# Six moves in a written-out order: an attention and expert-routing kernel on one core

## The chip, the cores and the metric

The kernel runs on 1 core of one Trainium2 chip. The metric is the device time of one execution in microseconds (us); less is better. The kernel before takes 195.74 us, the median of 3 runs (195.73 to 195.97).

## The reference

Two stages, one after the other. First an attention with pooled keys and values, for 8 batches of 8 heads, 576 queries and 64 columns a head; then a routed two-layer product of the 4608 rows that come out.

```python
k_p = k.reshape(B, H, 72, 8, D).mean(axis=3)          # 576 keys pooled to 72; v_p likewise
attn = softmax(q @ k_p.T / 8)
x = (attn @ v_p) as rows of 512                       # 576 rows for each batch
logits = normalized(x) @ normalized(expert_emb).T / tau
e = argmax(logits); gate = softmax(logits)[e]
out[row] = gate * (relu(x[row] @ w1[e]) @ w2[e])      # w1 512x1024, w2 1024x512, 8 experts
```

## The kernel before, in words

The kernel takes the 8 batches in turn and bets that all rows of a batch want one expert, which it guesses from the mean of the pooled values. It loads that expert's two weight arrays while the attention runs. A check at the end (`PR`, `PP`, `PX`) repeats a batch for which the guess was wrong.

Each batch is cut into steps, which are functions with a name and a batch number. Five lists in `TABLES` (L41 on), one for each of PE (TensorE), DVE (VectorE), ACT (ScalarE), POOL (GpSimd) and SP (SyncE), hold their names in the order in which that engine gets them. An engine runs its list strictly in order, so a step that waits holds up all that is behind it. `Plan.order` goes through the lists with an estimated time for each step; from that it takes two things only: which buffer a step gets (`Plan.free`: of the rings that the step allows, the slot that is reckoned free first), and how many dummy products (`keep_warm`, L959) are put ahead of a PE step in the first 62 us.

PSUM has two wide tiles (`pa`, 1024 columns, `psum`) and four narrow ones (`pb`, 512 columns, `bank`). Scores (`SC`) take both wide tiles at once; `PV` takes a wide one; all other PE steps take any of the six:

```python
tiles = [Buf(psum), Buf(psum)]          # SC
px = [Buf(psum)]                        # PV, from batch 1's on
p = Buf(bank, psum)                     # H, Y and the rest
```

The steps that the change and the prediction speak of, for batch b (`H3.4.0` is step H of batch 3, column block 4, row half 0):

- POOL: `V`, `K`, `Q`, `W1`, `W2` issue the loads of values, keys, queries and the two weight arrays; `PK` reads the guessed expert, which `GD` on DVE has found. `NA` takes the square root of the row norms (L446).
- DVE: `KA` and `KB` fold the 8 keys of a group into one (L506, L513), `VA` and `VB` the values. `QT` transposes queries (L605), four a batch. `KE` copies the transposed pooled keys (L632). `XM` divides the attention's output by its sums and gives x (L411, L412). `RE` finds the largest logit (L441 to L443), `NB` scales logits by the norms (L449 to L451), `ND` makes the gates.
- PE: `KT` transposes pooled keys (L616). `SC` makes scores from `KE` and `QT` (L646, L658). `PV` multiplies by the values (L725). `XT` transposes x (L420, L426). `RT` makes the logits (L435). `H` is a first-layer product of 4 matmuls (L822), `Y` a second-layer product for 128 rows (L834), `YL` that of the last 64 rows (L841).
- ACT and DVE share: `HE` takes the relu of an `H` out of PSUM (L828 on ACT, L830 on DVE), `XE` copies an `XT` (L743), `YE`, `YF` and `YG` scale a `Y` by its gate (L847, L849). A PSUM tile is free again only when this has been done.
- ACT alone: `EX` is the exponential of scores (L666, L674). `SQ` sums the squares of x (L754), one a chunk of rows; `NA` needs all five of a batch. `NC` is the exponential of logits (L813) and needs `NB`.

Batch 7, the last, has no work of a next batch beside it: its x is transposed by DMA (`XD`), and its 16 `H`, then `YL7` and the four `Y7`, end the kernel.

Of the kernel before, what the change touches and what calls it, by code (L numbers as in the profile page):

```python
# [44 lines left out]
H0.3.1 H0.4.1 GL1 H0.1.0 SC1.0.0 H0.0.1 H0.7.1 SC1.0.1 SC1.1.1 Y0.2 SC1.1.0 YL0 PV1.0 PV1.1 Y0.1  # L45
XT1.0 PV1.4 Y0.0 PV1.2 XT1.4 PV1.3 XT1.1 Y0.3 XT1.2 GM2 XT1.3 GL2 H1.5.0 H1.7.0 H1.4.0 H1.6.0
H1.5.1 H1.3.0 H1.1.0 H1.1.1 H1.2.0 KT2 RT1 H1.3.1 SC2.0 H1.4.1 H1.7.1 H1.2.1 H1.0.0 PV2.0 H1.0.1
H1.6.1 XT2.0 SC2.1 Y1.1 PV2.1 KT3 YL1 SC2.2 Y1.3 PV2.3 PV2.2 Y1.0 XT2.1 PV2.4 XT2.3 XT2.2 Y1.2
XT2.4 SC3.0 H2.2.0 RT2 H2.0.0 H2.1.0 H2.4.0 H2.0.1 H2.5.0 SC3.1 H2.5.1 H2.4.1 H2.2.1 H2.1.1
H2.6.0 GM4 GM3 H2.3.0 PV3.1 GL3 H2.7.0 H2.3.1 H2.6.1 H2.7.1 SC3.2 GL4 YL2 PV3.0 PV3.2 Y2.2 XT3.0  # L50
XT3.1 PV3.4 XT3.2 Y2.3 Y2.0 PV3.3 KT4 Y2.1 XT3.3 SC4.0 XT3.4 H3.3.0 H3.4.0 RT3 SC4.1 H3.2.0
H3.0.0 H3.3.1 H3.5.0 SC4.2 H3.1.0 H3.6.0 PV4.2 H3.7.0 H3.4.1 PV4.3 H3.1.1 PV4.0 H3.0.1 H3.6.1
H3.2.1 PV4.1 H3.7.1 XT4.0 H3.5.1 XT4.1 GM5 PV4.4 XT4.2 XT4.3 YL3 XT4.4 Y3.0 GL5 RT4 H4.7.0
H4.7.1 H4.5.0 H4.6.1 Y3.1 H4.5.1 Y3.2 Y3.3 H4.1.0 KT5 H4.6.0 H4.0.0 H4.3.0 SC5.0 H4.4.0 H4.0.1
# [8 lines left out]
""",  # L63
    "DVE": """
PRE GC0 GD0 VA0 QT0.0.0 QT0.0.1 KE0.0 KE0.1 QT0.1.0 QT0.1.1 VB0 XM0.0.0 XM0.1.0 XM0.0.1 XM0.1.1
XM0.3 XM0.2 XM0.4 VA1 VB1 RE0 GC1 KA1 KB1 HE0.5.1 KE1 QT1.0.0 QT1.0.1 GD1 QT1.1.0 QT1.1.1 GE0
HE0.0.1 HE0.1.1 NB0 ND0 YF0 XM1.0 XM1.1 VA2 XM1.4 VB2 KA2 XM1.2 XM1.3 GC2 KB2 HE1.5.0 XE1.3 GD2
HE1.4.0 QT2.0.0 QT2.0.1 QT2.1.1 QT2.1.0 KE2 RE1 HE1.3.1 NB1 HE1.1.1 XM2.0 GE1 KA3 KB3 XM2.1 ND1
QT3.0.0 QT3.0.1 QT3.1.1 KE3 XM2.3 YF1 XM2.2 XE2.1 XM2.4 QT3.1.0 XE2.2 VA4 VB4 RE2 HE2.0.0 GE2
HE2.4.0 HE2.1.0 HE2.5.0 VA3 VB3 NB2 GC4 GC3 GD3 XM3.1 HE2.3.1 HE2.6.1 ND2 GD4 YF2 XM3.0 QT4.0.0  # L70
XM3.2 QT4.0.1 KA4 XM3.4 KB4 QT4.1.0 XM3.3 QT4.1.1 KE4 YE2.1 XE3.3 XE3.4 RE3 HE3.4.0 VA5 VB5
XM4.2 HE3.0.0 XM4.3 XM4.0 XM4.1 XE4.0 HE3.5.1 NB3 XM4.4 QT5.0.0 GC5 GE3 QT5.1.0 ND3 RE4 GD5
QT5.1.1 QT5.0.1 YF3 KA5 VA6 HE4.5.0 VB6 KB5 HE4.6.1 GE5 KE5 VA7 HE4.3.0 NB4 YE3.3 HE4.4.0 KA6
GE4 HE4.1.1 ND4 QT6.0.0 KB6 YE4.3 GC6 QT6.1.1 YF4 XM5.2 XM5.0 GD6 XM5.4 XE5.0 XM5.1 KE6 XE5.2
XM5.3 QT6.1.0 VB7 QT6.0.1 HE5.5.0 HE5.2.0 RE5 QT7.0.0 HE5.1.0 GE6 QT7.1.1 GC7 GD7 HE5.4.0
# [19 lines left out]
XE5.3 YE4.1 EX6.0.0 EX6.0.1 HE5.5.1 SQ5.2 HE5.2.1 HE5.6.0 HE5.3.0 SQ5.0 EX6.1.0 HE5.4.1 EX6.1.1  # L95
HE5.3.1 HE5.7.0 HE5.0.0 HE5.1.1 HE5.0.1 SQ5.1 EX6.2.1 EX6.2.0 NC5 YE5.2 YG5 SQ6.2 XE6.2 SQ6.1
SQ6.3 YE5.0 XE6.4 SQ6.4 XE6.3 EX7.0.1 EX7.0.0 HE6.4.1 EX7.1.1 HE6.6.0 EX7.1.0 HE6.3.1 EX7.2.1
EX7.2.0 HE6.1.1 HE6.0.0 HE6.2.1 SQ6.0 NC6 SQ7.2 YE6.0 YE6.2 SQ7.1 HE7.3.0 HE7.6.0 YG6 SQ7.0
SQ7.3 SQ7.4 HE7.2.0 HE7.1.0 HE7.6.1 HE7.0.1 NC7 HE7.2.1 HE7.3.1 HE7.7.1 HE7.4.1 HE7.1.1 YG7
YE7.2 YE7.1.1  # L100
""",
    "POOL": """
V0.0 V0.1 K0.0 K0.1 Q0.0 Q0.1 V1.0 V1.1 PK0 W10 K1 Q1.0 W20 V2 K2 PK1 W11 Q2.0 NA0 K3 W21 Q3.0
# [1128 lines left out]
```

## Time and profile before

| what | value |
|---|---|
| median of 3 runs | 195.74 us |
| profiled execution | 196.42 us |
| its span | 194.6 us |
| PE busy | 186.9 us (96%), 2174 matmuls |
| DVE busy | 145.9 us (75%) |
| ACT busy | 126.6 us (65%) |
| POOL busy | 42.4 us (22%) |
| loads issued by POOL (q0) | 28.85 MB, 87.0% of 16 DMA engines' span |

The profile cuts the span into 40 equal slices; a digit is the busy share in tenths, and 9 is 90% or more:

```profile
PE   6999999999999999998999999999999999999991
DVE  1257888589978998879669999999798836863730
ACT  4017896776876998585987767727983787078410
PEclk9999999999999999999999999999999999999998
DMA  3999999999999999999999999999999991449843
```

PE counts as busy nearly throughout; matmuls overlap in the record, so what it loses shows only as short idle stretches ahead of single groups. PEclk is the granted clock of PE. The rest of the time between the span and the profiled execution's own time lies around the span.

### The profile page before, as it was taken

To read this page: it belongs to the slowest core of one execution; us is meant where nothing else is said; L and a number is where in the kernel's file an instruction comes from. 1 tells how busy PE (TensorE), PEld (TensorE's weight loads), DVE (VectorE), ACT (ScalarE), POOL (GpSimd) and SP (SyncE) were. 2 spreads that over 40 slices of the span, in tenths; PEclk is the share of its full clock that TensorE was granted. 3 is DMA by queue.
4 is the path that set the end of the run, shared out by engine and by line. 5 is a ranking of instruction groups with operands and counts; after the bars stand their busy time and mean duration, and the time that the engine had idled before them with its cause. 6 is when DMAs were issued, how large, how long until landed. Compare 5 with 4: busy or idle time off the path is not lost.

```text
span 194.6 us, 5502 instructions
## 1 busy us (share of the span) xinstructions
PE 186.9 (96%) x2174; PEld 127.2 (65%) x2175; DVE 145.9 (75%) x418; ACT 126.6 (65%) x288; POOL 42.4 (22%) x60
## 2 busy tenths in 40 slices
PE   6999999999999999998999999999999999999991
PEld 4775786556875677654786657667774778557651
DVE  1257888589978998879669999999798836863730
ACT  4017896776876998585987767727983787078410
POOL 7544000910371002350024332030140000202000
PEclk9999999999999999999999999999999999999998
DMA  3999999999999999999999999999999991449843
GB/s 38 179 207 202 206 212 206 179 207 208 209 208 210 207 211 203 141 191 206 214 196 218 261 212 226 249 192 203 251 262 231 214 317 63 97 148 344 298 138 115
DMA packets 30335, 39.30 MB, mean 202 GB/s; under 512 B 6616, under 2 KB 17112, under 8 KB 30304
## 3 DMA queue, kind: packets, MB, share of 16 engines
q0 software_dynamic: 21792, 28.85, 87.0%
q1 hardware_dynamic: 8288, 9.85, 15.5%
q8 instruction: 18, 0.29, 0.6%
q10 hardware_dynamic: 224, 0.20, 0.3%
q14 instruction: 13, 0.11, 0.2%
HBM read 61.88 MB, written 9.44 MB: 367 GB/s over the span
## 4 chain that ended last, share of the span: by engine, by line
PE 56%; DMA 19%; DVE 13%; issue 4%; POOL 3%; ACT 2%; POOLq 0%; DVEq 0%
PE pb L822 17%; DMA kr<-in_k_dram 15%; PE pb L834 13%; PE pa L834 4%; DMA qq<-in_q_dram 4%; PE pa L822 4%; DVE qT L605 3%; DVE x L412 3%; PE pa L658 3%; PE pa L725 3%; PE pb L841 2%; DVE kr L506 2%; PE pa L646 2%; PE pb L959 2%; POOL vr L362 1%
## 5 line engine op out<-in xcount | busy, mean ns | idle before, releaser
L822 PE MATMUL pb<-xt,w 128*128 128x288 f16 (+2 forms) x404 | 58.3, 286 | 0.2 <-ACT hT L828 0.2
L822 PEld LDWEIGHTS <-w 128*128 128x128 f16 x512 | 47.1, 98 | 13.6 <-issue 2.1
L834 PE MATMUL pb<-w,hT 128*128 128x512 f16 x208 | 48.7, 379 | 0.0
L834 PEld LDWEIGHTS <-hT 128*128 128x128 f16 x248 | 22.9, 98 | 24.8 <-issue 0.8
L666 ACT ACTIVATE at<-pa 72x792 f16<-72x792 f32 (+1 forms) x36 | 27.6, 803 | 9.4 <-PE pa L658 7.7
L828 ACT ACTIVATE hT<-pb 128x288 f16<-128x288 f32 (+2 forms) x66 | 24.9, 408 | 6.2 <-PE pb L822 5.4
L412 DVE TENSOR_TENSOR x<-pa,r_all 128x512 f16<-128x512 f32 x38 | 26.3, 691 | 1.4
L754 ACT ACTIVATE sq<-x 128x512 f16<-128x512 f16 x40 | 25.2, 629 | 1.5 <-DVE x L412 1.2
L605 DVE STREAM_TRANSPOSE qT<-qq 128x576 f16<-128x576 f16 x32 | 23.5, 758 | 2.0 <-DMA qq<-in_q_dram 2.0
L847 ACT ACTIVATE y<-pb,gm_all 128x512 f32<-128x512 f32 (+1 forms) x26 | 16.1, 627 | 9.5 <-PE pb L834 7.9
L446 POOL TENSOR_TENSOR ssq_all<-ssq_all,half_c 128x5 f32<-128x5 f32 x8 | 9.5, 1187 | 52.1 <-ACT sq L754 52.1
L830 DVE TENSOR_SCALAR hT<-pb 128x288 f16<-128x288 f32 (+1 forms) x35 | 15.3, 450 | 4.0 <-PE pb L822 3.8
L725 PEld LDWEIGHTS <-at 72*128 72x128 f16 x320 | 14.2, 98 | 4.7 <-issue 1.8
L822 PE MATMUL pa<-xt,w 128*128 128x288 f16 (+2 forms) x108 | 17.0, 286 | 0.0
L385 POOL DMA_DIRECT2D w<-in_moe_w_dram x8 | 5.5, 684 | 49.8 <-DVE hT L830 25.4
L959 PE MATMUL pb<-ones_m 128*128 128x256 f16 x97 | 14.3, 302 | 1.5 <-DVE half_c L966 1.5
L725 PE MATMUL pa<-vpx,at 72*128 72x65 f16 x304 | 15.3, 194 | 0.1
L506 DVE TENSOR_TENSOR vr<-vr 72x2048 f16<-72x2048 f16 (+1 forms) x16 | 15.1, 942 | 0.4 <-DMA vr<-in_v_dram 0.3
L506 DVE TENSOR_TENSOR kr<-kr 72x2048 f16<-72x2048 f16 (+1 forms) x14 | 13.2, 944 | 1.1 <-DMA kr<-in_k_dram 1.0
L959 PEld LDWEIGHTS <-ones_m 128*128 128x128 f16 x113 | 11.1, 106 | 4.1 <-DVE half_c L966 1.1
L411 DVE RECIPROCAL r_all<-pa 128x8 f32<-128x8 f32 x38 | 7.6, 200 | 7.6 <-PE pa L725 7.1
L743 ACT COPY xt<-pb 128x512 f16<-128x512 f16 x18 | 10.3, 584 | 3.1 <-PE pb L420 3.0
(132 smaller groups left out, 229.2 us busy)
## 6 DMA issues: line engine op xcount, KB each, us to landing
w<-in_moe_w_dram POOLq DMA_DIRECT2D x16, 1024.0 KB, 15.4
out_dram<-y SPq DMA_DIRECT2D x31, 256.0 KB, 6.0
kr<-in_k_dram POOLq DMA_DIRECT2D x7, 576.0 KB, 18.5
qq<-in_q_dram POOLq DMA_DIRECT2D x7, 576.0 KB, 17.4
vr<-in_v_dram POOLq DMA_DIRECT2D x6, 576.0 KB, 20.8
out_dram<-y SPq DMA_DIRECT2D x15, 64.0 KB, 5.7
qq<-in_q_dram POOLq DMA_DIRECT2D x2, 288.0 KB, 8.7
vr<-in_v_dram POOLq DMA_DIRECT2D x1, 512.0 KB, 6.3
```

Of the source, the lines that this page charges most:

```text
L412: nc.vector.tensor_tensor(out=x[:, ts(i, np_)], in0=pxv[:, :, 1:129].rearrange("p a (r d) -> p a r d", d=D), in1=rv.unsqueeze(3).to_broadc ...
L506: nc.vector.tensor_tensor(out=t[:, :, 0:m], in0=t[:, :, 0:m], in1=t[:, :, m:2 * m], op=ALU.add)
L605: nc.vector.transpose(out=qT.tile[:, a].rearrange("p t c e -> p (t c e)")[:, cols], in_=qq.tile[:, a, cols]),
L666: nc.scalar.activation(out=t.tile[:, :, p0 * T:p1 * T].rearrange("g z (p t) -> g z p t", t=T), in_=p.tile[0:G].rearrange("g (z c) -> g z c ...
L725: nc.tensor.matmul(out=px[h // 2 // np_].tile[:, o:o + 65], lhsT=at[h % 4 // 2].tile[:, h % 2 * NQ + h // 4, c0:c0 + 128], rhs=vp.tile[:, ...
L754: nc.scalar.activation(out=sq, in_=x.tile.rearrange("p a r d -> p (a r d)"), func=AF.Square, accum_out=ssq_all[:, b, c:c + 1])
L822: nc.tensor.matmul(out=p[:, 0:c1 - c0], lhsT=w1v[:, kk, w // 2, w % 2, :], rhs=xt[:, kk, c0:c1], start=(kk == 0), stop=(kk == 3))
L828: nc.scalar.activation(out=dst, in_=src, func=AF.Relu)
L830: nc.vector.tensor_scalar(out=dst, in0=src, scalar1=0.0, scalar2=None, op0=ALU.max)
L834: landing[f"Y{c}"] = nc.tensor.matmul(out=p, lhsT=hT[w][:, ts(c, 128)], rhs=w2[:, w // 2, w % 2, :], start=(w == 0), stop=(w == 7))
L847: nc.scalar.activation(out=dst, in_=src, func=AF.Copy, scale=g)
L959: nc.tensor.matmul(out=p[:, 256:512], lhsT=ones_m[:, 0:128], rhs=ones_m[:, 0:256], start=True, stop=True)
```

## The change

Six places of three lists are changed; nothing else. No step is added or taken away.

- PE, batch 2: `SC2.1` goes ahead of `XT2.0`.
- PE, batches 2 to 4: `Y2.1` goes ahead of `KT4`, and `XT3.4` ahead of `SC4.0`.
- DVE, batch 1: `QT1.0.0` goes ahead of `KE1`.
- DVE, batches 3 and 4: `QT4.1.0` and `XM3.4` go ahead of `KA4`, and `KB4` follows `KA4` directly.
- DVE, batches 3 and 4: `XM4.4` goes ahead of `NB3`.
- ACT, batch 7: `HE7.2.0` and `HE7.1.0` go ahead of `SQ7.0`, `SQ7.3` and `SQ7.4`.

```diff
     "PE": """
...
-H1.6.1 XT2.0 SC2.1 Y1.1 PV2.1 KT3 YL1 SC2.2 Y1.3 PV2.3 PV2.2 Y1.0 XT2.1 PV2.4 XT2.3 XT2.2 Y1.2
+H1.6.1 SC2.1 XT2.0 Y1.1 PV2.1 KT3 YL1 SC2.2 Y1.3 PV2.3 PV2.2 Y1.0 XT2.1 PV2.4 XT2.3 XT2.2 Y1.2
...
-XT3.1 PV3.4 XT3.2 Y2.3 Y2.0 PV3.3 KT4 Y2.1 XT3.3 SC4.0 XT3.4 H3.3.0 H3.4.0 RT3 SC4.1 H3.2.0
+XT3.1 PV3.4 XT3.2 Y2.3 Y2.0 PV3.3 Y2.1 KT4 XT3.3 XT3.4 SC4.0 H3.3.0 H3.4.0 RT3 SC4.1 H3.2.0
...
     "DVE": """
...
-XM0.3 XM0.2 XM0.4 VA1 VB1 RE0 GC1 KA1 KB1 HE0.5.1 KE1 QT1.0.0 QT1.0.1 GD1 QT1.1.0 QT1.1.1 GE0
+XM0.3 XM0.2 XM0.4 VA1 VB1 RE0 GC1 KA1 KB1 HE0.5.1 QT1.0.0 KE1 QT1.0.1 GD1 QT1.1.0 QT1.1.1 GE0
...
-XM3.2 QT4.0.1 KA4 XM3.4 KB4 QT4.1.0 XM3.3 QT4.1.1 KE4 YE2.1 XE3.3 XE3.4 RE3 HE3.4.0 VA5 VB5
-XM4.2 HE3.0.0 XM4.3 XM4.0 XM4.1 XE4.0 HE3.5.1 NB3 XM4.4 QT5.0.0 GC5 GE3 QT5.1.0 ND3 RE4 GD5
+XM3.2 QT4.0.1 QT4.1.0 XM3.4 KA4 KB4 XM3.3 QT4.1.1 KE4 YE2.1 XE3.3 XE3.4 RE3 HE3.4.0 VA5 VB5
+XM4.2 HE3.0.0 XM4.3 XM4.0 XM4.1 XE4.0 HE3.5.1 XM4.4 NB3 QT5.0.0 GC5 GE3 QT5.1.0 ND3 RE4 GD5
...
     "ACT": """
...
-EX7.2.0 HE6.1.1 HE6.0.0 HE6.2.1 SQ6.0 NC6 SQ7.2 YE6.0 YE6.2 SQ7.1 HE7.3.0 HE7.6.0 YG6 SQ7.0
-SQ7.3 SQ7.4 HE7.2.0 HE7.1.0 HE7.6.1 HE7.0.1 NC7 HE7.2.1 HE7.3.1 HE7.7.1 HE7.4.1 HE7.1.1 YG7
-YE7.2 YE7.1.1
+EX7.2.0 HE6.1.1 HE6.0.0 HE6.2.1 SQ6.0 NC6 SQ7.2 YE6.0 YE6.2 SQ7.1 HE7.3.0 HE7.6.0 YG6 HE7.2.0
+HE7.1.0 SQ7.0 SQ7.3 SQ7.4 HE7.6.1 HE7.0.1 NC7 HE7.2.1 HE7.3.1 HE7.7.1 HE7.4.1 HE7.1.1 YG7 YE7.2
+YE7.1.1
```

Around these, unchanged, DVE's list ends for batch 7 with `RE7 NB7 HE7.0.0 HE7.5.0 HE7.4.0 ND7 HE7.7.0 HE7.5.1`, and PE's goes `H7.3.0 H7.6.0 H7.2.0 H7.1.0 RT7 H7.6.1 H7.0.1 H7.3.1 H7.2.1 H7.5.0 H7.0.0 H7.4.0 H7.4.1 H7.7.0 H7.7.1 H7.5.1 H7.1.1 PP YL7 Y7.2 Y7.3 Y7.0 Y7.1.0 Y7.1.1`.

## Rows read from the trace of the kernel before

**Rows 1.** Busy us (instructions) by stretch: PE, PEld, DVE, ACT, POOL, PEclk, DMA, GB/s:

```profile
84.00:107.00 23.00, 22.10 (x279) 15.16 (x276) 18.62 (x46) 18.33 (x43) 4.71 (x7) 1.00 1.17 208
107.00:172.00 65.00, 64.99 (x755) 43.21 (x751) 53.95 (x156) 42.75 (x97) 9.64 (x11) 1.00 0.97 208
```

**Rows 2.** PE's timeline, 87 to 93: start, us, engine, line, out<-in, [idle before]:

```profile
88.61 0.44 PE L616 MATMUL pa<-ident_h,kp 72*128 72x72 f16 x4 [0.55 <-DVE kp L513]
88.89 1.89 PE L834 MATMUL pb<-w,hT 128*128 128x512 f16 x8
...
91.20 0.57 PE L658 MATMUL pa<-qT,kpT 32*72 32x198 f16 x16 [0.19 <-DVE kpT L632]
91.70 0.29 PE L426 MATMUL pb<-ident_h,x 128*128 128x64 f16 x4
91.82 1.14 PE L822 MATMUL pb<-xt,w 128*128 128x288 f16 x8
```

**Rows 3.** DVE's timeline, 83 to 92.5 (KA4, KE4, YE2.1):

```profile
85.58 1.22 DVE L506 TENSOR_TENSOR kr<-kr 72x2048 f16<-72x2048 f16 x1 [1.05 <-DMA kr<-in_k_dram]
...
90.88 0.27 DVE L632 COPY kpT<-pa 128x288 f16<-128x288 f16 x1
91.07 0.73 DVE L849 TENSOR_SCALAR y<-pb,gm_all 128x512 f32<-128x512 f32 x1
```

**Rows 4.** POOL's timeline, 74 to 84 (issue of batch 3's w1):

```profile
79.16 0.82 POOL L385 DMA_DIRECT2D w<-in_moe_w_dram  x1 [5.06 <-DVE hT L830]
```

**Rows 5.** DMAs issued from 79 to 80: KB, us from issue to landing:

```profile
w<-in_moe_w_dram POOLq DMA_DIRECT2D x1, 1024.0 KB, 12.4
```

**Rows 6.** PE's timeline, 31 to 58 (SC1.0.0, SC2.0, XT2.0):

```profile
32.42 0.44 PE L646 MATMUL pa<-qT,kpT 32*72 32x288 f16 x8 [0.18 <-DVE mx_all L580]
...
53.61 0.57 PE L658 MATMUL pa<-qT,kpT 32*72 32x198 f16 x16
...
57.60 0.40 PE L420 MATMUL pb<-ident_h,x 128*128 128x128 f16 x4
```

**Rows 7.** DVE's timeline, 49 to 58 (QT2's four, XM2.0's product):

```profile
50.61 2.76 DVE L605 STREAM_TRANSPOSE qT<-qq 128x576 f16<-128x576 f16 x4 [0.45 <-DMA qq<-in_q_dram]
...
56.85 0.69 DVE L412 TENSOR_TENSOR x<-pa,r_all 128x512 f16<-128x512 f32 x1
```

**Rows 8.** PE's timeline, 102.9 to 110 (PV4.4, XT4.4, H4.5.0):

```profile
102.98 0.42 PE L725 MATMUL pa<-vpx,at 72*128 72x65 f16 x8
...
105.00 0.29 PE L426 MATMUL pb<-ident_h,x 128*128 128x64 f16 x4 [0.16 <-DVE x L412]
...
108.45 0.65 PE L822 MATMUL pa<-xt,w 128*128 128x288 f16 x4
```

**Rows 9.** DVE's timeline, 102.4 to 108.6 (first of NB3, last of RE4):

```profile
103.19 0.45 DVE L449 TENSOR_SCALAR ssq_all<-ssq_all 128x5 f32<-128x5 f32 x1
...
108.01 0.19 DVE L443 TENSOR_TENSOR lg_all<-pa,lmax_all 128x40 f32<-128x40 f32 x1
```

**Rows 10.** POOL's timeline, 101 to 105 (a load of queries is issued):

```profile
102.90 0.76 POOL L368 DMA_DIRECT2D qq<-in_q_dram  x1
```

**Rows 11.** ACT's timeline, 174.5 to 182.7 (HE7.2.0, HE7.1.0):

```profile
177.60 0.41 ACT L828 ACTIVATE hT<-pb 128x288 f16<-128x288 f32 x1
177.91 0.40 ACT L828 ACTIVATE hT<-pa 128x288 f16<-128x288 f32 x1
```

**Rows 12.** POOL's timeline, 168 to the end (NA7):

```profile
177.65 1.16 POOL L446 TENSOR_TENSOR ssq_all<-ssq_all,half_c 128x5 f32<-128x5 f32 x1 [11.08 <-ACT sq L754]
```

**Rows 13.** DVE's timeline, 178 to 182.6 (first of NB7, HE7.0.0):

```profile
178.85 0.17 DVE L449 TENSOR_SCALAR ssq_all<-ssq_all 128x5 f32<-128x5 f32 x1 [2.34 <-POOL ssq_all L446]
...
179.39 0.45 DVE L830 TENSOR_SCALAR hT<-pa 128x288 f16<-128x288 f32 x1
```

**Rows 14.** PE's timeline, 176 to 183.6 (H7.5.0; H7.7.0 and H7.7.1):

```profile
178.06 0.65 PE L822 MATMUL pb<-xt,w 128*128 128x288 f16 x4 [0.21 <-ACT hT L828]
...
180.02 1.14 PE L822 MATMUL pa<-xt,w 128*128 128x288 f16 x8
```

## The prediction

> **What bounds the kernel now.** I read three views in this order. First the busy time by stretch: between 107 and 172 us TensorE (PE) is busy for 64.99 of 65 us at full clock, so nothing is to be won there, and between 84 and 107 us it is busy for 22.10 of 23 [rows 1]. What an order can give or take is therefore a handful of short TensorE stalls. Second, TensorE's timeline, where each stall stands in brackets ahead of the group that waited, with the engine that ended it. Third, the timelines of VectorE (DVE), ScalarE (ACT) and GpSimd (POOL) at those places, to see what would be late next. The profiled execution took 196.42 us with a span of 194.6; the median of the runs shown is 195.74, that is 0.68 less. I work in differences against the profiled one and apply them to the median.
>
> Four small stalls lie under the edits in the later half: 0.55 ahead of KT4, 0.19 ahead of SC4.0 [rows 2], 0.16 ahead of XT4.4 [rows 8], 0.21 ahead of H7.5.0 [rows 14]. Two more lie in the earlier half: 0.18 ahead of SC1.0.0, and at XT2.0 (57.60), which starts 0.06 after XM2.0 ends [rows 6, 7]. Taken at face value the six places are worth about 1.4 us. I think most of it does not arrive.
>
> **QT1.0.0 ahead of KE1 (DVE).** VectorE no longer idles for KT1, so both transposes of head group 0 end up to 0.45 us earlier and SC1.0.0 can start 0.2 to 0.35 us earlier. But 21 us later SC2.0 (53.61) starts right after KE2, behind four transposes that began at 50.61, when the q rows had landed [rows 6, 7]. That landing comes out of a queue that is busy all along (the page's DMA line shows nine tenths or more in each slice here), and SC2.0 cannot move with it. Bounds: 0 to -0.35 us. I take 0, since the row at 50.61 names the DMA.
>
> **SC2.1 ahead of XT2.0 (PE).** XT2.0 waits for XM2.0's output. SC2.1 needs both wide PSUM tiles, and PV2.0 holds one of them until the same XM2.0 has read it. So SC2.1 waits for 57.54 as well, and the pair ends when it did. Its exponentials start about 0.3 us sooner, but PV2.1, which uses them, sits behind Y1.1 on TensorE anyway. Bounds: -0.1 to +0.1. I take 0.
>
> **KT4, Y2.1, XT3.4, SC4.0 (PE) and QT4.1.0, XM3.4, KA4, KB4 (DVE).** These go together. VectorE idles 1.05 us for k's landing ahead of KA4 [rows 3]. QT4.1.0 and XM3.4 now fill that, and the rest of its list comes 1.05 us sooner: KE4, which stood right behind QT4.1.1 at 90.88, could start at about 89.85. On TensorE, Y2.1 takes KT4's place. Groups overlap by 0.16 in the rows (KT4 runs 0.44 from 88.61, Y2.1 starts at 88.89), so Y2.1 starts at 88.06 - 0.16 = 87.9 and KT4 follows at 87.9 + 1.89 - 0.16 = 89.6, ending at about 90.0. So KE4 (0.27) now waits for KT4 and ends at 90.3.
>
> Now two new limits come in. (a) Any first- or second-layer product takes whichever PSUM buffer is reckoned free first. With XM3.4 moved up, the wide tile that it frees is the first free one when Y2.1 is placed, and SC4.0 needs both wide tiles. So SC4.0 would wait for YE2.1, which starts 0.19 after KE4 and takes 0.73 [rows 3]: about 90.95. SC4.0 then starts at 91.0 and, at 0.50 a piece (91.20 to 91.70 in the same view), hands over at 91.5. (b) The next group, H3.3.0, is the first that reads batch 3's first-layer weights. Their load was issued at 79.16 and landed 12.4 us later, at 91.56 [rows 4, 5]. H3.3.0 started at 91.82 [rows 2], so it can come forward by 0.24 us at most, whatever else is ready. Of the 0.74 us of visible idle, 0.24 is real. Bounds: 0 (if the chain over YE2.1 ends 0.3 later than reckoned) to -1.0 (if neither limit holds). I take -0.24.
>
> **XM4.4 ahead of NB3 (DVE).** XT4.4 waited for XM4.4, which stood behind NB3 on DVE [rows 8, 9]. XM4.4 itself can start once PV4.4's result is there (102.98 + 0.42 = 103.40 [rows 8]), with NB3's three instructions behind it; XT4.4 then follows YL3 with no stall. Start to start this is worth 0.23 us. What is late next is VectorE's own list: it idles 0.2 us for PV4.4, NB3 comes behind, and RE4 (end 108.20) must free the tile of H4.5.0 (108.45) [rows 8, 9]. With the 0.24 from before, TensorE would be at H4.5.0 at 107.98, and RE4 would end between 107.90 and 108.18. So between 0 and -0.23 of this term passes. The row that decides is NB3's first instruction: 0.45 us, against 0.17 for the same instruction at 178.85 [rows 9, 13]. It ran while POOL was issuing a DMA, and both ended together (103.64 and 103.66) [rows 9, 10]. Moved 0.9 us later it may or may not meet the next issue. I take -0.07, which leaves -0.31 in all.
>
> The Trainium skill (SBUF — State Buffer, section "SBUF: two separate sides") explains such a pair: GpSimd and a VectorE instruction in a two-port mode exclude each other for the whole instruction. The rows agree in this one place. By the rule alone, NB3 pays again if another issue is running when it starts, and the time would be 195.95; with no collision it would be 195.7.
>
> **HE7.2.0 and HE7.1.0 ahead of SQ7.0, SQ7.3, SQ7.4 (ACT).** H7.5.0 waited for the buffer that HE7.2.0 drains (177.60) [rows 11, 14]; drained ahead of the squares, it is free near 175.7, and the stall goes: 178.06 becomes about 177.7, start to start 0.38 better. The price: SQ7.4 now ends two drains later, 2 x 0.31 (the next drain starts 0.31 after the one at 177.60) less up to 0.13, so 0.47 to 0.60. NA7 on POOL waits for it (177.65, ended by ACT's squares), NB7 on DVE waits for NA7 (178.85), and HE7.0.0 is queued behind NB7 on DVE (179.39, 0.45 long) [rows 11 to 13]. H7.7.0 takes the buffer that HE7.0.0 frees at 179.84 and started at 180.02 [rows 14]: a slack of 0.18. No other buffer helps. There are six, and ahead of H7.7.0 stand H7.3.1, H7.2.1, H7.5.0, H7.0.0, H7.4.0 and H7.4.1, whose drains are queued behind NB7 on DVE, or on ACT behind NC7, which itself waits for NB7. So H7.7.0 moves to 180.36 to 180.49, +0.34 to +0.47, and the 0.38 gained before it is eaten in the same stall. The products behind it follow at 0.49 each (1.14 for two against 0.65 for one [rows 14]), then YL7 and the four last products with no cover, so this goes to the end. I take +0.43.
>
> **Sum.** 0 + 0 - 0.24 - 0.07 + 0.43 = +0.12 us: 196.54 for a profiled execution, 195.9 as a median. I call within 0.2% (0.39 us, so 195.35 to 196.13) no change, which is about what a measurement of this kernel can tell.
>
> **Rivals.**
> 1. The tail's new wait does not come, because NA7, NB7 and HE7.0.0 are not that tight. Then the 0.38 stays: -0.31 - 0.38 = -0.69, 195.05. For it: the stall at H7.5.0 is real. Against it: the slack is 0.18 and all six buffers hang on NB7. Chance 0.12.
> 2. The weights of batch 3 or the buffer of Y2.1 are no limit. Then H3.3.0 comes at about 90.8, -1.0; VectorE's wait for v's landing and its list at 104 to 108 let some 0.8 of it pass; with +0.43 that is -0.4, 195.3. For it: a landing is read from semaphores and may be a little off. Against it: H3.3.0 must wait for that load in any order. Chance 0.13.
> 3. Slower: Y2.1 in the wide tile costs all of the middle. SC4.0 waits for YE2.1, behind KE4, behind KT4, which Y2.1 now holds back. If YE2.1 ends past 91.25 instead of 90.95, H3.3.0 is no earlier than before, and the late stall of +0.43 stands alone: 196.2; at 91.6 it is 196.5. For it: three hand-overs in a row, each with a wait. Against it: 0.3 us of margin. Chance 0.20.
> 4. The early gain (0.35 at SC1.0.0) passes after all, if q lands earlier because GD1, and with it POOL, comes sooner: 195.5. Against it: loads issued before were still queued. Chance 0.05.
>
> My forecast has 0.50. Its own range is 195.6 to 196.1. The range for 8 in 10 reaches to rivals 1 and 3: 195.0 to 196.4. Faster is rivals 1 and 2 with a little less than half a tenth of the rest, 0.28; slower is three quarters of rival 3 and the upper edge of the forecast, 0.19; no change 0.53.
>
> **What the changed profile would show.** H7.5.0 starts right behind H7.2.1, and the idle stands ahead of H7.7.0 instead, ended by DVE, 0.6 to 0.8 us from start to start. KT4's idle is gone, and an idle of some tenths ended by DVE (YE2.1) or a DMA stands ahead of SC4.0 or H3.3.0, which starts 12.4 us after its weights were issued. XT4.4 has no idle. SC2.0 still starts 3.0 us after the q rows landed. I am wrong if H7.7.0 follows H7.4.1 with no idle, or if H3.3.0 starts more than 0.5 us ahead of 91.8.

## The result and the profile after

The changed kernel takes 196.6 us in the median, the kernel before 195.7: ratio 1.0055, 95% interval 1.0039 to 1.0071, that is +0.76 to +1.39 us. I had forecast 195.9 with a range of 195.0 to 196.4, so it was slower than the range allows. A second comparison gave 1.0040 (1.0019 to 1.0062).

The first profile of the changed kernel is of an execution of 199.61 us, whose granted clock was 0.50 (1.2 GHz) from 20 to 25 us; I read the second one, of 196.38 us (span 194.5). It is shown below. Its page begins:

```profile
span 194.5 us, 5509 instructions
## 1 busy us (share of the span) xinstructions
PE 186.8 (96%) x2176; PEld 127.8 (66%) x2177; DVE 145.7 (75%) x418; ACT 126.6 (65%) x288; POOL 42.5 (22%) x60
```

TensorE's waits from 60 us on (engine, line, what it waited for: us in total, times, longest), first in the profiled execution of the kernel before:

```profile
PE pa L616 <- DVE kp L513: 0.5, 1, 0.5
PE pb L822 <- ACT hT L828: 0.2, 1, 0.2
PE pa L658 <- DVE kpT L632: 0.2, 1, 0.2
PE pb L426 <- DVE x L412: 0.2, 1, 0.2
```

and in the changed kernel:

```profile
PE pa L822 <- DVE hT L830: 0.8, 1, 0.8
PE pa L658 <- DVE y L849: 0.4, 1, 0.4
```

All four waits of before are gone, and the two new ones are those that the prediction named: H7.7.0 waits for HE7.0.0, and SC4.0 for YE2.1. Put against the profiled execution of before, at 196.42, the changed one is 0.04 us shorter. Put against the median of before it is 0.7 longer. That difference is what the experiments are about.

The middle in the changed kernel, TensorE from 87 to 92 us; it answers to [rows 2]:

```profile
87.52 0.42 PE L725 MATMUL pa<-vpx,at 72*128 72x65 f16 x8
87.78 1.89 PE L834 MATMUL pa<-w,hT 128*128 128x512 f16 x8
89.50 0.30 PE L616 MATMUL pb<-ident_h,kp 72*128 72x72 f16 x4
...
90.27 0.28 PE L658 MATMUL pa<-qT,kpT 32*72 32x198 f16 x2
90.92 0.56 PE L658 MATMUL pa<-qT,kpT 32*72 32x198 f16 x14 [0.38 <-DVE y L849]
91.42 1.03 PE L822 MATMUL pb<-xt,w 128*128 128x288 f16 x7
```

Y2.1 (87.78) now writes a wide tile, pa. SC4.0 gets as far as its first two matmuls at 90.27, then waits for the wide tile until VectorE has drained Y2.1. From PV3.3 (87.52) to H3.3.0 (91.42) is 3.90 us. In the profiled execution of before it was 87.65 to 91.82, 4.17. I call this the stretch below.

VectorE at the same place; it answers to [rows 3]:

```profile
85.80 1.93 DVE L506 TENSOR_TENSOR kr<-kr 72x2048 f16<-72x2048 f16 x2
...
89.91 0.31 DVE L632 COPY kpT<-pb 128x288 f16<-128x288 f16 x1
90.13 0.74 DVE L849 TENSOR_SCALAR y<-pa,gm_all 128x512 f32<-128x512 f32 x1
```

KA4 starts without the idle of 1.05, KE4 ends at 90.22 (I had 90.3) and YE2.1 at 90.87 (I had 90.95).

The tail in four timelines; they answer to [rows 11 to 14]. ACT (HE7.2.0, HE7.1.0, then the first of the squares):

```profile
174.75 0.41 ACT L828 ACTIVATE hT<-pb 128x288 f16<-128x288 f32 x1
175.05 0.40 ACT L828 ACTIVATE hT<-pa 128x288 f16<-128x288 f32 x1
175.48 0.63 ACT L754 ACTIVATE sq<-x 128x512 f16<-128x512 f16 x1
```

POOL (NA7, the sum of squares):

```profile
177.79 1.16 POOL L446 TENSOR_TENSOR ssq_all<-ssq_all,half_c 128x5 f32<-128x5 f32 x1 [11.82 <-ACT sq L754]
```

DVE (first of NB7; HE7.0.0 with HE7.5.0):

```profile
178.99 0.17 DVE L449 TENSOR_SCALAR ssq_all<-ssq_all 128x5 f32<-128x5 f32 x1 [3.08 <-POOL ssq_all L446]
...
179.53 0.81 DVE L830 TENSOR_SCALAR hT<-pa 128x288 f16<-128x288 f32 x2
```

PE (H7.5.0 with H7.0.0, H7.4.0 with H7.4.1, H7.7.0):

```profile
177.08 1.14 PE L822 MATMUL pa<-xt,w 128*128 128x288 f16 x8
178.06 1.14 PE L822 MATMUL pb<-xt,w 128*128 128x288 f16 x8
180.04 0.65 PE L822 MATMUL pa<-xt,w 128*128 128x288 f16 x4 [0.83 <-DVE hT L830]
```

H7.5.0 starts with no idle, and the idle stands ahead of H7.7.0, ended by HE7.0.0, 1.00 us start to start (180.04 less 178.06, less 2 x 0.49), where I had forecast 0.6 to 0.8. The first square begins 0.73 us after HE7.2.0 did (175.48 less 174.75): that is the price of two drains ahead of it, 0.30 for the first and 0.43 for the second.

### The profile page after: what moved, and what is told of

Read it like the earlier page. It is cut to its first block, busy times and chain, and to the rows that moved or that the text cites. A ratio compares the mean times of both kernels' runs of the same rounds, so it can differ in the third digit from the quotient of the medians.

```text
span 197.8 us, 5509 instructions
## 1 busy us (share of the span) xinstructions
PE 189.7 (96%) x2176; PEld 130.1 (66%) x2177; DVE 145.9 (74%) x418; ACT 126.7 (64%) x288; POOL 42.5 (21%) x60
## 4 chain that ended last, share of the span: by engine, by line
PE 76%; issue 7%; DVE 5%; DMA 5%; POOL 2%; ACT 1%; POOLq 1%; DVEq 0%
PE pb L822 24%; PE pb L834 16%; PE pa L822 6%; PE pa L834 5%; DMA qq<-in_q_dram 5%; PE pa L658 4%; PE pa L725 4%; PE pb L841 4%; PE pb L420 3%; PE pb L959 2%; PE pa L646 2%; DVE x L412 1%; PE pb L435 1%; PE pb L863 1%; DVE vr L506 1%
## 5 line engine op out<-in xcount | busy, mean ns | idle before, releaser
L834 PE MATMUL pb<-w,hT 128*128 128x512 f16 x192 | 44.9, 379 | 0.0
L847 ACT ACTIVATE y<-pb,gm_all 128x512 f32<-128x512 f32 (+2 forms) x27 | 16.5, 620 | 14.2 <-PE pb L834 7.9
L822 PE MATMUL pa<-xt,w 128*128 128x288 f16 (+2 forms) x112 | 17.7, 286 | 0.8 <-DVE hT L830 0.8
L725 PEld LDWEIGHTS <-at 72*128 72x128 f16 x320 | 15.2, 101 | 4.6 <-issue 1.6
L959 PE MATMUL pb<-ones_m 128*128 128x256 f16 x97 | 16.1, 326 | 1.5 <-DVE half_c L966 1.5
L830 DVE TENSOR_SCALAR hT<-pb 128x288 f16<-128x288 f32 (+1 forms) x33 | 14.5, 451 | 3.9 <-PE pb L822 3.8
L725 PE MATMUL pa<-vpx,at 72*128 72x65 f16 x304 | 16.0, 198 | 0.0
L959 PEld LDWEIGHTS <-ones_m 128*128 128x128 f16 x115 | 12.1, 114 | 4.9 <-issue 1.2
```

The source lines that it names most:

```text
L725: nc.tensor.matmul(out=px[h // 2 // np_].tile[:, o:o + 65], lhsT=at[h % 4 // 2].tile[:, h % 2 * NQ + h // 4, c0:c0 + 128], rhs=vp.tile[:, ...
L822: nc.tensor.matmul(out=p[:, 0:c1 - c0], lhsT=w1v[:, kk, w // 2, w % 2, :], rhs=xt[:, kk, c0:c1], start=(kk == 0), stop=(kk == 3))
L830: nc.vector.tensor_scalar(out=dst, in0=src, scalar1=0.0, scalar2=None, op0=ALU.max)
L834: landing[f"Y{c}"] = nc.tensor.matmul(out=p, lhsT=hT[w][:, ts(c, 128)], rhs=w2[:, w // 2, w % 2, :], start=(w == 0), stop=(w == 7))
L847: nc.scalar.activation(out=dst, in_=src, func=AF.Copy, scale=g)
L959: nc.tensor.matmul(out=p[:, 256:512], lhsT=ones_m[:, 0:128], rhs=ones_m[:, 0:256], start=True, stop=True)
```

## The experiments

Each was timed in five rounds beside the kernel before, except the third profile of the kernel before, which is one execution. Where the edit is one of order, the diff shows the places in the engine's list. The runs fall into three groups, and the kernel before has another median in each: 195.78 beside the first four, 196.40 beside the middle alone, the narrow buffer, the change without the middle and the mended tail, 195.71 beside the last two. So ratios can be compared across the groups, and times cannot.

**The changed kernel again, and the kernel before again.**

> The changed kernel once more, for a profile without the low clock that its first one had between 20 and 30 us. Theory A (the tail alone makes it slower, all other edits give what the first profile shows, 0.27 + 0.23 + 0.12): no place ahead of 170 us is later than in the kernel before, and H7.7.0 stands 0.6 us later against its neighbours. Theory B (something ahead of 40 us costs about 0.5 to 1 us, which the delay of 3 us in the first profile covered): the profile shows PE at SC1.0.0 or SC2.0 later than before. Time 196.6 by both.

Measured: 196.53, ratio 1.0040 (1.0019 to 1.0062); its rows are above. From 32 us to the tail no group of TensorE is more than 0.05 us later than in the profile of before, save XT2.0 and KT4, which the edits put behind another group. So far it is as theory A has it: H7.3.0 is 0.61 us earlier (172.63 against 173.24) and the end is level. But then a kernel of 196.38 stands level with one of 196.42 whose median is 195.7, and theory A does not explain the 0.7.

> The kernel before once more, for a second profile of it: the first one was of an execution of 196.42, 0.7 above the median. If the 0.7 stands ahead of 30 us (Theory B: the start differs from execution to execution), the second profile has its groups from 60 us on at other times by a constant; by Theory A they agree within 0.2 us. Time 195.6, ratio 1.000.

Measured: 195.73, ratio 1.0002 (0.9976 to 1.0027). In this profile, of an execution of 197.92 us, all of TensorE's groups from 24 us on stand 2.6 us later than in the first one, up to PV3.3 at 90.25:

```profile
90.25 0.42 PE L725 MATMUL pa<-vpx,at 72*128 72x65 f16 x8
90.51 0.29 PE L616 MATMUL pa<-ident_h,kp 72*128 72x72 f16 x4
...
93.31 1.15 PE L822 MATMUL pb<-xt,w 128*128 128x288 f16 x8
```

KT4 has no idle, and H3.3.0 is at 93.31, only 1.49 later: the stretch took 3.06 us, not 4.17. So 1.11 us of the stretch that I had taken for the kernel's own was waiting for landings in that one execution. k had been issued 2.6 later and landed 2.3 earlier (83.28 against 85.56).

**The tail alone, and the change without the tail.**

```diff
 # ACT
-SQ7.0 SQ7.3 SQ7.4 HE7.2.0 HE7.1.0
+HE7.2.0 HE7.1.0 SQ7.0 SQ7.3 SQ7.4
```

> The kernel before with the edit on ACT alone. Theory A: +0.6 us (H7.5.0 0.38 earlier, H7.7.0 0.99 later from there), 196.2, ratio 1.003. My forecast's own term would give +0.43. Theory B's rest would be seen in the run without this edit. If the tail costs all of the +1.0, 196.6.

Measured: 196.24, ratio 1.0019 (0.9987 to 1.0052), too wide to say much. The profile is sharp: H7.5.0 comes 0.38 earlier and H7.7.0 0.99 later from there, +0.61 to the end, theory A's value. The stretch is 3.06.

> The changed kernel with the edit on ACT undone. Theory A: the gains stay, -0.4 to -0.6 against the kernel before, 195.0 to 195.2, ratio 0.997. Theory B: the loss in the early part stays, +0.3 to +0.5, 195.9 to 196.1.

Measured: 195.99, ratio 1.0027 (0.9992 to 1.0063): the gain of 0.4 to 0.6 us that theory A wanted lies outside the interval, so the tail is not all of the loss. The changed kernel took 196.53 beside it, 0.54 more, near the 0.61 of the tail. Its profile has the stretch at 3.90 and the idle of 0.21 ahead of H7.5.0 as before. Theory B wanted the loss ahead of 40 us; from 12 to 40 us no group of TensorE is more than 0.05 us later than in the kernel before, so theory B fell, and theory C (the middle) took its place.

**The middle alone.**

```diff
 # PE
-KT4 Y2.1 XT3.3 SC4.0 XT3.4
+Y2.1 KT4 XT3.3 XT3.4 SC4.0
 # DVE
-KA4 XM3.4 KB4 QT4.1.0
+QT4.1.0 XM3.4 KA4 KB4
```

> The kernel before with the middle edits alone (Y2.1 ahead of KT4, XT3.4 ahead of SC4.0, QT4.1.0 and XM3.4 ahead of KA4). Theory C: from PV3.3 to H3.3.0 the kernel before needs 3.06 us when k has landed in time and up to 4.17 when it lands late as in its first profile, the edit makes it 3.90 whatever k does; most executions have k early, so the edit costs: +0.4 to +0.8, 196.0 to 196.4, ratio 1.002 to 1.004, 3.90 in the profile. Rival (the first profile is like the rest): -0.27 us, 195.35.

Measured: 196.66, ratio 1.0030 (0.9990 to 1.0069); the time alone decides nothing, the profile does: a stretch of 3.90 (87.60 to 91.50). TensorE at the place:

```profile
90.35 0.28 PE L658 MATMUL pa<-qT,kpT 32*72 32x198 f16 x2
91.01 0.56 PE L658 MATMUL pa<-qT,kpT 32*72 32x198 f16 x14 [0.38 <-DVE y L849]
91.50 0.91 PE L822 MATMUL pb<-xt,w 128*128 128x288 f16 x6
```

Its weights had landed at 89.88, so they do not hold H3.3.0; YE2.1 does, by way of SC4.0.

**The middle with Y2.1 in a narrow buffer.**

```diff
-            p, y = Buf(bank, psum), Buf(y_r)
+            p, y = Buf(*((bank,) if (b, c) == (2, 1) else (bank, psum))), Buf(y_r)
```

> The same middle edits, but Y2.1 is given a narrow PSUM buffer, so that SC4.0 doesn't wait for YE2.1. Theory C with the wait on YE2.1 as its larger half: the stretch from PV3.3 to H3.3.0 falls from 3.90 to 3.3 to 3.5, +0.1 to +0.4 against the kernel before, 0.4 to 0.5 better than the middle edits alone. Rival (the weights of batch 3 hold H3.3.0): the stretch stays at 3.8 to 3.9 and the time is that of the middle edits alone.

Measured: 195.93, ratio 0.9997 (0.9958 to 1.0035). TensorE at the place (this execution began 1.4 us late, so all stands later):

```profile
89.05 0.42 PE L725 MATMUL pa<-vpx,at 72*128 72x65 f16 x8
89.30 1.89 PE L834 MATMUL pb<-w,hT 128*128 128x512 f16 x8
...
91.80 0.57 PE L658 MATMUL pa<-qT,kpT 32*72 32x198 f16 x16
92.30 1.16 PE L822 MATMUL pb<-xt,w 128*128 128x288 f16 x8
```

SC4.0 runs in one piece, and the stretch is 3.25: 0.65 of the 0.84 us between 3.06 and 3.90 is the wait for the wide tile. The rest is that SC4.0 still follows KE4 (its end 91.74, SC4.0 91.80) and KT4, which now come behind Y2.1. The times agree: timed beside each other, all 12 executions of the middle alone took 196.25 or more, and 9 of the 12 with the narrow buffer 196.09 or less; the medians are 0.73 apart. The rival, that the weights hold H3.3.0, did not come true here (they landed at 90.89, H3.3.0 is at 92.30).

**The change without the middle.**

```diff
 # the changed kernel, with these put back
-Y2.1 KT4 XT3.3 XT3.4 SC4.0
+KT4 Y2.1 XT3.3 SC4.0 XT3.4
-QT4.1.0 XM3.4 KA4 KB4
+KA4 XM3.4 KB4 QT4.1.0
```

> The changed kernel with the middle edits undone. By the profiles the rest is worth -0.12 (SC1.0.0), -0.12 (SC2.1), -0.23 (XT4.4) and +0.61 (tail). Theory C: +0.1 to +0.4 against the kernel before (the first two may be lost to k's landing), 195.7 to 196.0, 0.5 to 0.8 better than the changed kernel. Rival (the middle edits gain 0.27): 196.8, worse than the changed kernel.

Measured: 196.01, ratio 0.9983 (0.9942 to 1.0023): no longer clear of the kernel before, where the whole change is. The interval holds the expected +0.1 to +0.4 us, and its upper end is +0.45, so the rival (a loss of more than 1 us) did not come true. The profile has a stretch of 3.06 with k in time and no wait at KT4.

**The kernel before a third time.**

> The kernel before once more, for a profile of an execution near its median. Theory C: at 195.5 to 195.8 us k has landed before 84.8, VectorE idles less than 0.4 us for it, and PV3.3 to H3.3.0 takes 3.06 to 3.4 us. Rival: 4.17 there too, and the 0.7 us that the first profiled execution was above the median lie elsewhere.

Measured: 195.93. k had landed at 84.46, and KA4 (84.60) starts straight behind QT4.0.1, with no idle; KT4 has none either. The stretch is 3.69 all the same. TensorE, with the issue of batch 3's weights behind it (KB, us to landing):

```profile
87.79 0.42 PE L725 MATMUL pa<-vpx,at 72*128 72x65 f16 x8
88.05 0.29 PE L616 MATMUL pa<-ident_h,kp 72*128 72x72 f16 x4
88.18 1.89 PE L834 MATMUL pb<-w,hT 128*128 128x512 f16 x8
...
90.22 0.57 PE L658 MATMUL pa<-qT,kpT 32*72 32x198 f16 x16
90.72 0.29 PE L426 MATMUL pb<-ident_h,x 128*128 128x64 f16 x4
91.48 0.91 PE L822 MATMUL pb<-xt,w 128*128 128x288 f16 x6 [0.47 <-DMA w<-in_moe_w_dram]
```

```profile
w<-in_moe_w_dram POOLq DMA_DIRECT2D x1, 1024.0 KB, 12.1
```

So there are two landings that can hold this stretch in the order of before, k's at KT4 and the weights' at H3.3.0. Theory C had only the first, and its 3.06 to 3.4 was missed; the second is the prediction's limit (b), met here in the kernel before. In the first profile both were late: the weights landed at 91.54, 3.89 after PV3.3, so with k in time the stretch would still have been 3.89 or more.

**The tail mended, the three good edits alone, and both.**

```diff
 # ACT, beside the edit of the tail
-NC7 HE7.2.1 HE7.3.1
+HE7.3.1 HE7.2.1 NC7
 # DVE
-NB7 HE7.0.0 HE7.5.0 HE7.4.0 ND7 HE7.7.0 HE7.5.1
+HE7.5.0 HE7.0.0 HE7.4.0 NB7 HE7.7.0 HE7.5.1 ND7
```

> The kernel before with the ACT edit, and HE7.5.0, HE7.0.0 and HE7.4.0 ahead of NB7, HE7.7.0 and HE7.5.1 ahead of ND7 on DVE, HE7.3.1 and HE7.2.1 ahead of NC7 on ACT. If the drains queued behind NB7 and NC7 are what holds H7.7.0, both stalls of the tail go: -0.3 to -0.4 against the kernel before (195.2 to 195.4, ratio 0.998). Rival (the squares that now end 0.74 later hold the end by way of the gates in any order): +0.1 to +0.6.

Measured: 195.19, ratio 0.9940 (0.9899 to 0.9980), that is -0.4 to -2.0 us; the expected -0.3 to -0.4 lies at the edge of it, and I rest on the profile for the size. DVE (HE7.5.0 with HE7.0.0, HE7.4.0, NB7):

```profile
177.40 0.95 DVE L830 TENSOR_SCALAR hT<-pa 128x288 f16<-128x288 f32 x2 [1.86 <-PE pa L822]
178.38 0.46 DVE L830 TENSOR_SCALAR hT<-pb 128x288 f16<-128x288 f32 x1
178.75 0.16 DVE L449 TENSOR_SCALAR ssq_all<-ssq_all 128x5 f32<-128x5 f32 x1
```

PE (H7.4.0, H7.4.1 and H7.7.0 in one row, with no idle):

```profile
177.69 1.63 PE L822 MATMUL pb<-xt,w 128*128 128x288 f16 x12
```

VectorE stood idle for 3.08 us ahead of NB7 in the changed kernel, with HE7.5.0 behind it; that could have started near 177.8, an estimate from the 0.69 between H7.5.0 (176.71) and HE7.5.0 (177.40) in this run. With three drains ahead, NB7 starts 0.17 us after POOL's end (177.41 + 1.17 = 178.58) instead of 0.04, and no product of batch 7 waits. From H7.2.1 to the end this is 0.37 us better than before (the end is 1.35 earlier than in the first profile, H7.2.1 0.98), where the edit as made is 0.61 worse. So the rival did not come true: with the drains out of their way, the squares being later costs the end nothing.

> The three edits alone that the profiles show as gains (QT1.0.0 ahead of KE1, SC2.1 ahead of XT2.0, XM4.4 ahead of NB3): -0.47 us if all of it lasts, 195.15; -0.22 if k's landing takes the first two back, 195.4. My forecast gave these three -0.07 together.

The edits are QT1.0.0 ahead of KE1, SC2.1 ahead of XT2.0 and XM4.4 ahead of NB3, as in the change. Measured: 195.73, ratio 0.9987 (0.9956 to 1.0018), not to be told from no change by the time. In the profile all three last to the end: 0.14 at SC1.0.0, 0.11 at SC2.1, 0.23 at XT4.4, and the profiled execution took 195.03.

> The changed kernel without its middle edits and with the tail's drains moved as in the run of the tail alone (HE7.5.0, HE7.0.0, HE7.4.0 ahead of NB7, HE7.7.0 and HE7.5.1 ahead of ND7, HE7.3.1 and HE7.2.1 ahead of NC7). If the parts add up: -0.15 (SC1.0.0) -0.10 (SC2.1) -0.22 (XT4.4) -0.37 (tail) = -0.84 us against the kernel before, 194.8, ratio 0.9957. Rival (the first two are given back at k's landing, as KT4 waits for it in some executions): -0.6, 195.0.

These three with the mended tail. Measured: 195.09, ratio 0.9956 (0.9922 to 0.9990), -0.2 to -1.5 us, which fits the sum of -0.84 and the rival's -0.6 alike. It is clear of the kernel before; the changed kernel and the mended tail alone were not timed beside it, so the times do not show what the three edits add to the tail.

## Why the prediction was wrong

**The step that failed** is in its first paragraph: "I work in differences against the profiled one and apply them to the median." The profiled execution stood 0.68 above the median, and the excess lay in the very stretch that the change rearranges: 4.17 us there, 3.06 where no landing is late. In the order of before, eight profiled executions have a stretch of 4.17 (the first), 3.69 (the third) and 3.06 (the other six: the second of the kernel before, and one each of five kernels with its middle). In the changed order it is 3.90 in all four. So the middle edits trade a wait for a landing, which six of these eight don't have, for a wait on YE2.1, which all four have. Against the first execution that is -0.27; against the six it is +0.84; against the mean of the eight, 3.28, it is +0.62. Three of the six (the second of the kernel before, the tail alone, the three edits with the mended tail) stand 1.4 to 3.1 us late at PV3.3, while their weights landed from 90.68 to 90.87, within the 90.30 to 91.54 of the other five; a late execution meets its loads more easily. Without those three the mean is 3.41, and the price of the middle +0.49.

- **The middle, -0.24.** Each limit was right: Y2.1 took the wide tile, KE4 waited for KT4, SC4.0 waited for YE2.1 to 90.87, and against the profiled execution it came to -0.27. As a term on the median it has the wrong sign, by every one of these means. Rival 3 had this mechanism, but asked whether YE2.1 would end past 91.25, a bound from the same one execution; without a landing wait H3.3.0 stands at 90.85 (in the profile of the mended tail), SC4.0 at 90.22, and YE2.1 need only end past 90.2 to cost.
- **The tail, +0.43.** The mechanism was right: all six buffers are drained behind NB7 or NC7. The size was short by 0.18. I priced two drains at 2 x 0.31, the spacing of a drain behind a drain, and took off 0.13 at most. A square behind a drain starts after 0.43, so NB7 moved by 0.73. H7.7.0 came 0.06 after HE7.0.0's end (179.98), so 0.12 of the slack of 0.18 was to be had, and the end moved by +0.61. My own working did not close either: 2 x 0.31 less 0.13 is 0.49, not 0.47, and 0.47 to 0.60 less 0.18 is 0.29 to 0.42, not 0.34 to 0.47.
- **XT4.4, -0.07.** It gave -0.23, as start to start. I expected RE4 to take back part. RE4's last step ended at 107.71 in the changed profile, 0.15 ahead of H4.5.0 (107.86). NB3's first instruction took 0.16 there, although POOL was issuing a DMA from 103.30 to 104.13. An issue that is running is not enough to make it long, then: in the profile of before the same instruction of NB0 took 0.17 (from 36.75) within an issue of 36.67 to 37.55. All seven profiles with XM4.4 behind NB3 have 0.44 or 0.45 there, all six with XM4.4 ahead of it have 0.16. So what the prediction worked out from the port rule of the Trainium skill (SBUF — State Buffer, section "SBUF: two separate sides"), that NB3 pays again if an issue is running when it starts, did not come true. No row shows who holds the ports, and what made the 0.45 stays open.
- **QT1.0.0, 0.** It gave -0.14, and SC2.0 did not take it back. The idle at 50.61 in [rows 7] that I took for a limit was a landing of that execution again: in the changed profile the four transposes begin at 50.07 with no idle, KE2 ends at 53.07, and SC2.0 follows at 53.60, 0.58 behind the product ahead of it, the same as in the kernel before (53.03 to 53.61): KE2 held it in neither. What I had not seen is that the plan puts one more warming product ahead of SC1.0.0 and one ahead of SC1.0.1 (2174 to 2176 matmul records); the first (32.20, 0.27 long) stands straight ahead of SC1.0.0 (32.41).
- **SC2.1, 0.** It gave -0.11: SC2.1 did part of its work (57.40, 0.74 long) in the tile that was free, and XT2.0 followed at 58.07.

One of the signs that I had named came true by luck: H3.3.0 starts 12.4 us after its weights were issued (91.42 less 79.03), but the weights had landed after 11.0, at 90.07, and YE2.1 made the 12.4.

The terms that the profiles show, -0.14 -0.11 +0.62 -0.23 +0.61, come to +0.75 us with the mean stretch of the eight, +0.62 with that of the five, +0.97 with 3.06. The two comparisons gave +1.08 (0.76 to 1.39) and +0.78 (0.37 to 1.21). What stays open is how often each landing is late over all executions, and with it the size of the middle's term between +0.49 and +0.84: eight are few, and I did not try to make a landing late on purpose.

## What to carry to other kernels

A stall on a transfer's landing in one profile may be a draw and not a property of the order: when the profiled execution stands above the median by about the size of the stall, price the edit with the stall and without it, and read a second profile. Here moving work ahead of a late operand paid only in an execution where it was late, and the new wait that it brought was there in all four profiles. Before putting work ahead of a chain, see what lies queued behind the chain on an idle engine: here the same edit cost 0.61 us with the drains behind NB7, and gave 0.37 with those behind NB7, ND7 and NC7 moved ahead.

## What the runs showed that I had not expected

The landing of a load did not move with its issue. Batch 3's weights, issued at 79.16, landed at 91.54; issued at 81.77 in the second profile of the same kernel, they landed at 90.68. k, issued at 56.33, landed at 85.56, and issued at 58.94, at 83.28. Issued within 0.3 us of each other (79.03 to 79.31), the weights took 11.0 us in the changed kernel and 12.1 in the third profile of the kernel before. That spread of about a microsecond is larger than every single term of this change. Over all 13 profiles these weights were issued from 78.94 to 82.25 and landed from 89.88 to 91.54.
